# A new order for attention and a mixture of adapters, with three pairs of pieces stored as one

## The chip, the core and the metric

The kernel runs on one core of one Trainium2 chip. The metric is the device time of one execution in microseconds; the median of four executions before the change is 254.44 us (254.34 to 254.68). A second number is the span of a profiled execution, from the first to the last instruction.

A core has five instruction streams. PE (TensorE) multiplies matrices, DVE (VectorE) and ACT (ScalarE) work on tiles and copy results out of PSUM, POOL (GpSimd) here issues the loads, and SP (SyncE) issues the stores. The 16 DMA engines of the core move the data; loads and stores have a queue each and share these engines.

## The reference, cut to what matters

Four batches of 6400 rows and 256 columns. Attention is taken across the columns: the Gram matrix of k and q over all 6400 rows of a batch, divided by the norms of the columns, goes through a softmax and gives a 256x256 matrix `a`; each row of v is multiplied by it. The result goes through eight small adapters of rank 16, of which each row takes its best two.

```python
qn = q / (np.linalg.norm(q, axis=1, keepdims=True) + 1e-06)
kn = k / (np.linalg.norm(k, axis=1, keepdims=True) + 1e-06)
s = kn.transpose(0, 2, 1) @ qn / tau
a = np.exp(s - s.max(-1, keepdims=True))
a /= a.sum(-1, keepdims=True) + 1e-09
x = (v @ a).reshape(B * S, D)
...
logits = x @ w_gate
topk = np.argpartition(-logits, K, axis=1)[:, :K]      # K = 2
w = softmax of the two logits
x + sum over the two of w * ((x @ A[e]) @ B[e])
```

## The kernel before

**Tiles.** A batch's 6400 rows lie as 128 partitions times 50 rows ("columns" of 256 numbers, 1 KB in DRAM, 512 bytes in SBUF since the loads convert to bf16). q and k are loaded in three parts of 17, 17 and 16 columns (`QK`), the first part of batch 0 with four columns ahead on other queues, and some parts in two transfers (`PARTS`). v is loaded in five pieces of 10 columns. There are six buffers for parts of q and k, three for pieces of v, four for transposed v (`vT`), and seven for results (`y`), each of one piece (`STORE`).

**Stages of a batch.** For each of the 50 columns, PE adds k's column times q's column to the Gram matrix in PSUM (L593). The squared norms come in one of two ways, by groups of columns: with PE as two more matmuls of 128 columns (L597 for k, L602 for q), or, for the groups listed in `OFF`, with ACT squaring (L615), DVE adding (L621, L627, L630) and a small matmul at the end (L636). A chain of short steps follows: diagonals (L663), an inverse square root (L677 to L693), scaling (L705, L710), exp (L715), sum and transposes (L722 to L735), the product of `a` with the gate and adapter weights (L742 to L757), and `a` itself (L763).

**Pieces.** Each piece of v is transposed by PE (L788) and copied to `vT`. Gate logits and the adapters' first products come in one of two ways: merged, in one run of 136-column matmuls (L812) that is copied out to `zl` before the gate can be worked out, for the pieces in `MERGED`; or apart, with 8-column matmuls for the logits first (L826) and 128-column matmuls for the products later (L879). DVE finds the two best in eight short steps (L845 to L868, one of ACT among them), multiplies (L890), PE transposes again (L902), and the output of two columns at a time is four matmuls of vT with `a` (L915) and two of the adapters' second weights (L920). ACT or DVE copies it to `y` (L769, L771). A store moves a piece of `y` to DRAM (L928); the last two pieces go out in three stores each (`FINE`).

**What sets the order.** Nothing is scheduled on the chip. `make_plan` writes down every step with an engine, or a choice of two, its cost in microseconds, its dependences, a rank, and the buffers that it takes and gives back. `Plan.run` plays them through: at each moment each engine takes the step of the lowest rank that is ready, loads go out in the order of `WORDS` as soon as their buffer is free, and two DMA queues share the bandwidth. The order in which it started the steps is the order in which the program is recorded, engine by engine. So every constant of that play (`LAT`, `ISSUE`, the costs in `make_plan`, `Clock` for PE's clock) can move any instruction. `warm` steps are matmuls of zeros (L777) that it puts in where PE has nothing to do.

**Queues.** POOL issues the loads one after another (L578): a load that waits for its buffer holds up all loads behind it. The buffer of a part of q or k is free when its Gram columns and squares are done, that of a piece of v when its last transpose is done. SP issues the stores in one order too. `HOLD` keeps some stores back until a load has landed, so that loads have the DMA to themselves: before the change by a small transfer into `scrap` that reads the loaded tile (L645), behind which the later stores stand.

The loads of the kernel before follow `WORDS` after the three parts of batch 0 ("q11" is the second part of q and k of batch 1, "v03" the fourth piece of v of batch 0):

```python
WORDS = ('q10 v00 v01 v02 q11 v03 q12 v04 v10 v11 q20 v12 v13 v14 q21 v20 v21 v22 q22 q30 '
         'q31 q32 v23 v24 v30 v31 v32 v33 v34')
```

## Time and profile before

| | |
|---|---|
| Median of four executions | 254.44 us |
| The profiled execution's own time | 254.68 us |
| Its span | 252.9 us |
| Mean granted TensorE clock | 0.975 |
| POOL's loads of v waiting for PE's transposes | 119.5 us in 12 waits |
| Instruction fetch (queue q8) | 18 packets, 0.29 MB |
| A v load of 640 KB, issue to landing, median | 18.1 us |
| A y store of 1280 KB, issue to landing, median | 16.8 us |
| First load of 512 KB (q, issued at 0.00) | 3.9 us |

How to read the profile's rows: busy time is given for each engine with its share of the span and the number of instructions. The rows of digits cut the span into 40 slices; a 9 means 90% or more. In the tables by stage the columns are the stretch, its length, the busy time of each engine with its number of instructions, the granted share of PE's clock, the mean busy share of the 16 DMA engines (packets overlap a little, so a full stage shows slightly over 1) and the bytes that they moved per time. A load counts there with the bytes that it writes to SBUF, half of what it reads. In the chain of waits a row is a start, a length and what it was. In the table of waits a row is who waited, for what, and then the sum, the number and the longest.

### The profile page before, as it was taken

The numbers are of one execution on the slowest core, as the hardware profiler recorded it, in microseconds if no ns is written. First come the engines' busy times: TensorE is split into PE (matmuls) and PEld (weight loads), VectorE is DVE, ScalarE is ACT, GpSimd is POOL, SyncE is SP. The second block draws the span as 40 slices with busy tenths as digits, with TensorE's granted clock in tenths as the row PEclk, the third lists the DMA queues.
The fourth block names the chain that finished last, engine by engine and source line by source line (L and its number), as shares of the span: only waits on it lengthen the run. The fifth ranks groups of instructions, "written<-read, shape, count | busy, mean of one in ns | idle before, by whom it ended". The sixth has DMA issues, their size and how long they took to land.

```text
span 252.9 us, 5852 instructions
## 1 busy us (share of the span) xinstructions
PE 221.4 (88%) x2357; PEld 195.1 (77%) x2357; DVE 192.8 (76%) x528; ACT 151.0 (60%) x269; POOL 27.0 (11%) x54
## 2 busy tenths in 40 slices
PE   0275997988999998989999999889999979999990
PEld 0163882776899998789899899779999768999980
DVE  0055589768988996888899898589898898888840
ACT  5454427444876665785667758362674846657670
POOL 7003010040002002000500100500000000000000
PEclk9999798699999999999999999999999999999998
DMA  8999999999999999999999999999999999999995
GB/s 252 217 217 209 212 221 214 212 219 212 218 215 217 316 284 295 264 212 222 211 213 220 216 217 213 216 210 321 312 253 353 330 330 323 339 390 426 399 405 225
DMA packets 11243, 66.70 MB, mean 264 GB/s; under 512 B 1360, under 2 KB 1744, under 8 KB 6608
## 3 DMA queue, kind: packets, MB, share of 16 engines
q0 software_dynamic: 6912, 38.80, 74.3%
q1 hardware_dynamic: 3968, 26.87, 26.1%
q10 hardware_dynamic: 336, 0.66, 0.7%
q8 instruction: 18, 0.29, 0.4%
q14 instruction: 9, 0.07, 0.1%
HBM read 78.91 MB, written 26.21 MB: 416 GB/s over the span
## 4 chain that ended last, share of the span: by engine, by line
PE 72%; DMA 12%; DVE 9%; ACT 2%; issue 2%; POOL 2%; DVEq 0%; POOLq 0%
PE Y_ps L915 17%; PE acc L593 14%; DMA qk<-in_k_dram 12%; PE Y_ps L920 8%; PE T_ps L788 7%; PE ZL_ps L812 6%; PE gzT_ps L902 5%; PE acc L597 4%; PE acc L602 3%; PE warm_ps L777 2%; PE n2p_ps L636 2%; DVE a_bf L763 2%; POOL qk L578 1%; PE Z_ps L879 1%; PE log_ps L826 1%
## 5 line engine op out<-in xcount | busy, mean ns | idle before, releaser
L593 PE MATMUL acc<-qk 128*128 128x256 bf16 x400 | 71.7, 289 | 16.3 <-DMA qk<-in_k_dram 9.1
L915 PE MATMUL Y_ps<-a_bf,vT 128*128 128x256 bf16 x400 | 60.0, 272 | 0.2 <-DVE acc_sb L710 0.2
L621 DVE TENSOR_TENSOR ssq<-ssq,sq 128x1280 f32<-128x1280 f32 (+1 forms) x27 | 43.4, 1606 | 19.6 <-ACT sq L615 19.6
L769 ACT COPY y<-Y_ps 128x512 f32<-128x512 f32 x79 | 46.1, 586 | 17.5 <-PE Y_ps L920 14.4
L593 PEld LDWEIGHTS <-qk 128*128 128x128 bf16 x400 | 35.3, 104 | 20.7 <-DMA qk<-in_k_dram 10.8
L615 ACT ACTIVATE sq<-qk 128x1280 f32<-128x1280 bf16 (+1 forms) x27 | 36.9, 1367 | 17.5 <-DVE ssq L621 16.6
L915 PEld LDWEIGHTS <-vT 128*128 128x128 bf16 x400 | 39.0, 98 | 4.7 <-issue 0.3
L920 PE MATMUL Y_ps<-ball,gzT 128*128 128x256 bf16 x200 | 38.2, 273 | 0.0
L597 PE MATMUL acc<-qk 128*128 128x128 bf16 x242 | 34.9, 226 | 0.0
L769 ACT COPY vT<-T_ps 128x512 f32<-128x512 f32 (+1 forms) x44 | 21.2, 510 | 12.8 <-PE T_ps L788 12.4
L788 PE MATMUL T_ps<-ident,v 128*128 128x128 f32 x200 | 27.5, 274 | 0.6 <-DVE waA_sb L757 0.4
L597 PEld LDWEIGHTS <-qk 128*128 128x128 bf16 x242 | 24.7, 102 | 3.9
L890 DVE TENSOR_TENSOR gz<-zl,gateg 128x256 bf16<-128x256 f32 x70 | 26.4, 445 | 0.3
L578 POOL DMA_DIRECT2D v<-in_v_dram x20 | 11.5, 575 | 132.8 <-PE T_ps L788 119.5
L602 PE MATMUL acc<-qk 128*128 128x128 bf16 x168 | 23.6, 223 | 0.0
L788 PEld LDWEIGHTS T_ps<-ident,v 128*128 128x128 f32 x200 | 22.3, 141 | 1.6 <-DVE waA_sb L757 0.6
L902 PE MATMUL gzT_ps<-ident,gz 128*128 128x128 f32 x100 | 20.9, 281 | 2.6 <-DVE gateg L868 1.4
L920 PEld LDWEIGHTS <-gzT 128*128 128x128 bf16 x200 | 19.6, 98 | 2.3
L812 PE MATMUL ZL_ps<-waA_sb,vT 128*128 128x136 bf16 x280 | 19.5, 223 | 1.7 <-DVE waA_sb L757 1.5
L812 PEld LDWEIGHTS <-vT 128*128 128x128 bf16 x280 | 17.7, 98 | 2.4 <-issue 2.1
L771 DVE COPY gzT<-gzT_ps 128x256 f32<-128x256 f32 (+1 forms) x40 | 15.0, 379 | 4.7 <-PE gzT_ps L902 3.1
L771 DVE COPY y<-Y_ps 128x512 f32<-128x512 f32 x21 | 14.5, 700 | 4.1 <-PE Y_ps L920 4.1
(80 smaller groups left out, 271.2 us busy)
## 6 DMA issues: line engine op xcount, KB each, us to landing
out_dram<-y SPq DMA_DIRECT2D x18, 1280.0 KB, 16.8
v<-in_v_dram POOLq DMA_DIRECT2D x20, 640.0 KB, 18.1
qk<-in_q_dram POOLq DMA_DIRECT2D x7, 1088.0 KB, 20.1
qk<-in_k_dram POOLq DMA_DIRECT2D x7, 1088.0 KB, 26.0
qk<-in_q_dram POOLq DMA_DIRECT2D x4, 512.0 KB, 19.4
qk<-in_k_dram POOLq DMA_DIRECT2D x4, 512.0 KB, 22.7
qk<-in_q_dram POOLq DMA_DIRECT2D x2, 1024.0 KB, 18.7
qk<-in_k_dram POOLq DMA_DIRECT2D x2, 1024.0 KB, 23.0
```

The lines of the kernel that those rows point to most:

```text
L593: nc.tensor.matmul(acc[ic][:, 0:256], kt[:, j, ic::CC], qt[:, j, :], start=c == 0, stop=False, skip_group_check=True)
L597: nc.tensor.matmul(acc[ic][:, 256:384], kt[:, j, ic::CC], kt[:, j, ic::CC], start=False, stop=False, skip_group_check=True)
L602: nc.tensor.matmul(acc[ic][:, 384:512], qt[:, j, ic * P:(ic + 1) * P], qt[:, j, ic * P:(ic + 1) * P], start=False, stop=c == NC - 1, skip_ ...
L615: nc.scalar.activation(out[:, 0:n, :], t[:, j:j + n, :], ACT.Square)
L621: nc.vector.tensor_tensor(out=t, in0=t, in1=held["sq", (w, b, g), ""][:, 0:n, :], op=OP.add)
L769: nc.scalar.copy(out, in_)
L771: nc.vector.tensor_copy(out, in_)
L788: nc.tensor.matmul(ps[:, j, :], vt[:, c + j, :].bitcast(FP32), W["ident32"], is_transpose=True, start=(j == 0), stop=(j == n - 1))
L812: nc.tensor.matmul(ps[:, j, :], vT_of(b, i, c + j)[:, :, ic], st[b]["waA"][:, ic, :], start=(j == 0 and ic == 0), stop=(j == n - 1 and ic ...
L902: nc.tensor.matmul(ps[:, j, :], pairs[:, j * P:(j + 1) * P], W["ident32"], is_transpose=True, start=(j == 0), stop=(j == n // 2 - 1))
L915: nc.tensor.matmul(ps[:, j, :], vT_of(b, i, c + j)[:, :, ic], st[b]["a"][:, ic, :], start=(j == 0 and ic == 0), stop=False, skip_group_che ...
L920: nc.tensor.matmul(ps[:, j, :], pair[:, :, j], W["B"], start=False, stop=(j == 1), skip_group_check=True)
```

## The change

The change does five things.

1. The play of the plan is another. DMA is no longer two streams that share by size: each transfer is eight rows per engine, two rings take turns row by row, a few rows are fetched ahead, and a landing takes longer the later it is. Costs of steps are other numbers, `Clock` uses other thresholds, and `HEAD`, the time at which software loads begin to move, is 5.05 instead of 2.6.
2. With it the constants of the order are others: `WORDS`, `HOLD`, `OFF` (31 entries instead of 35), `MERGED` (8 pieces instead of 14), `AHEAD`, `SQ`, `SAFE`.
3. `y` and `v` are each one tile with slots in place of a tile for each buffer, so that two neighbouring slots can be read by one store.
4. `PAIRS`: pieces 0 and 1 of batch 0, 0 and 1 of batch 1, and 2 and 3 of batch 2 lie in neighbouring slots and are stored in one transfer of 20 columns each, 20 KB per partition.
5. A held store has a dependence on the load itself (`add_manual_dep`) and the transfers into `scrap` are gone.

What is computed is the same: the same matmuls, with other pieces merged and other groups of squares on PE or on ACT and DVE. The loads keep their sizes; four columns of q and k of batch 0 go ahead as before.

```diff
-    WINDOW, FIRST, LOW, HIGH = 3.413, 0.31, 0.5, 0.8
+    WINDOW, FIRST, LOW, HIGH = 3.413, 0.31, 0.4, 0.8
...
-    SPARE = 1.0
+    SPARE = 1.5
...
-    LAT = 0.07
-    DMA_LAT = 1.8
+    TAIL = {"PE": 0.164, "DVE": 0.083, "ACT": 0.1}
+    LAT = 0.037
     ENGINES = ("PE", "DVE", "ACT", "POOL", "SP")
-    ISSUE = 0.55
-    ISSUE_LAT = 1.8
-    STORE_LAT = 1.4
+    ISSUE, ISSUE_LAT = 0.52, 1.8
+    STORE, STORE_LAT = 0.46, 0.85
     OUT = 8
+    PIPE, FETCH = 2.9, 1.005
+    ROW, SEM = (0.003, 0.012), (0.021, 0.006)
+    DMA_LAT, SPREAD, SKEW = 0.31, 0.6, 0.008
...
+        def fill():
+            nonlocal turn, ahead
+            while ahead < self.PIPE and (rings[0] or rings[1]):
+                turn = 1 - turn if rings[1 - turn] else turn
+                s = rings[turn][0]
+                if s.rows:
+                    s.rows -= 1
+                    us, last = s.size * self.FETCH + self.ROW[turn], None
+                else:
+                    rings[turn].pop(0)
+                    us, last = self.SEM[turn], s
+                pipe.append((us, last))
+                ahead += us
...
+PAIRS = {(0, 0), (1, 0), (2, 2)}
...
+def pieces(b, i):
+
+    return next((((b, j), (b, j + 1)) for j in (i - 1, i) if (b, j) in PAIRS), ((b, i),))
...
-    for kind, b, i in sorted(set(HOLD.values())):
-        part = [k for k in p.steps if k[:4] == ("load", kind, b, i)]
-        p.add(("hold", kind, b, i), {"SP": 0.3}, part[-1:], 0, size=0.01)
...
-WORDS = ('q10 v00 v01 v02 q11 v03 q12 v04 v10 v11 q20 v12 v13 v14 q21 v20 v21 v22 q22 q30 '
-         'q31 q32 v23 v24 v30 v31 v32 v33 v34')
-HEAD = 2.6
-LOAD = 0.304
+WORDS = ('v00 q10 v01 q11 v02 q12 v03 q20 q21 v04 v10 v11 q22 v12 v13 q30 v14 q31 v20 v21 v22 q32 v23 v24 v30 '
+         'v31 v32 v33 v34')
+HEAD = 5.05
+COL = 1.024 * 1.17647 / 32
 WARM = 150
-AHEAD = 2.7
+AHEAD = 3.4
...
+HOLD = {(0, 0): ('k', 3, 0), (0, 1): ('v', 0, 4), (0, 2): ('v', 3, 3), (0, 3): ('v', 3, 4), (1, 0): ('v', 2,
+        3), (1, 1): ('k', 1, 1), (1, 2): ('v', 2, 4), (1, 3): ('v', 3, 2), (1, 4): ('k', 3, 1), (2, 4):
+        ('v', 3, 3), (3, 2): ('v', 2, 3), (3, 3): ('v', 0, 1), (3, 4): ('k', 2, 1)}
...
+MERGED = {(0, 1), (0, 4), (1, 1), (1, 3), (1, 4), (2, 1), (2, 3), (2, 4)}
...
+    Y = sbuf.tile([P, STORE["y"] * PC, C], FP32, name="y")
+    VS = sbuf.tile([P, STORE["v"] * PC, C], BF16, name="v")
...
     def do_store(s, b, i, c, n):
         lo = i * PC + c
-        nc.sync.dma_start(out_v[b, :, lo:lo + n, :], held["y", (b, i), ""][:, c:c + n, :])
+        at_y = at["y", (b, i)] * PC + c
+        p = 0
+        for rows in SHARES if (b, i) in SPLIT else (P,):
+            r = nc.sync.dma_start(out_v[b, p:p + rows, lo:lo + n, :], Y[p:p + rows, at_y:at_y + n, :])
+            if (b, i) in HOLD and not p:
+                tc.add_manual_dep(r.ins, loaded[held_by(plan, b, i)],
+                                  mybir.DependencyInfo(mybir.DependencyClass.Sync, mybir.DependencyReason.DATA),
+                                  reason="held")
+            p += rows
```

In the program that this makes, SP's stores come in this order (batch.piece; in brackets the load whose landing a store is held for): 0.4; the pair 0.0 and 0.1 [k of q30]; 1.4 [k of q31]; 2.0; the pair 1.0 and 1.1 [v23]; 1.2 [v24]; 2.1; the pair 2.2 and 2.3; 1.3 [v32]; 0.2 [v33]; 2.4 [v33]; 0.3 [v34]; 3.0; 3.1; 3.2; and 3.3 and 3.4 in three stores each. Before it was 0.2; 0.1 [k of q12]; 0.3; 0.0 and 1.0 [k of q31]; then 2.0, 0.4, 1.1, 1.2, 1.3, 1.4 and 2.1 [k of q31 or q32]; 2.2 to 3.2 one by one; and 3.3 and 3.4 in three each. PE has 2357 matmuls before and 2506 after, of them 39 and 12 on zeros; the last eight pieces' outputs stand behind the last Gram matmul before, and the last seven after. DVE has 48 instructions fewer, ACT 22 more.

## The prediction

> **What bounds the kernel now.** I read the page first, then the busy time by stages, the chain of waits and the waits of the loads' queue.
>
> ```profile
> span 252.9 us, 5852 instructions
> ...
> PE 221.4 (88%) x2357; PEld 195.1 (77%) x2357; DVE 192.8 (76%) x528; ACT 151.0 (60%) x269; POOL 27.0 (11%) x54
> ...
> DMA  8999999999999999999999999999999999999995
> ...
> q0 software_dynamic: 6912, 38.80, 74.3%
> q1 hardware_dynamic: 3968, 26.87, 26.1%
> ...
> HBM read 78.91 MB, written 26.21 MB: 416 GB/s over the span
> ```
>
> The row DMA is full in every slice but the first and the last, and the two queues add up to 100.4% of 16 engines' span. No instruction engine comes near that. Loads read 78.9 MB and stores write 26.2 MB whatever the order, so a new order can win only idle DMA time, or lose more of it. The chain of waits gives PE 72%: PE works nearly all the time too, but not on the tightest resource. Where is the DMA idle? By stages:
>
> ```profile
> core 0: us, PE busy (x) PEld busy (x) DVE busy (x) ACT busy (x) POOL busy (x), PEclk, DMA share, GB/s
> ...
> 10.00:80.00 70.00, 59.22 (x543) 47.73 (x544) 50.29 (x113) 40.79 (x57) 8.46 (x15) 0.93 1.04 215
> 80.00:105.00 25.00, 24.15 (x273) 21.92 (x271) 21.33 (x65) 14.65 (x28) 2.94 (x6) 1.00 1.03 292
> ...
> 225.00:235.00 10.00, 10.00 (x130) 9.51 (x128) 9.10 (x29) 6.82 (x17) 0.00 (x0) 1.00 1.02 427
> 235.00:240.00 5.00, 5.00 (x58) 4.60 (x55) 4.36 (x15) 3.28 (x8) 0.00 (x0) 1.00 0.92 384
> ...
> 245.00:250.00 5.00, 1.55 (x15) 1.14 (x12) 0.00 (x0) 1.96 (x4) 0.00 (x0) 1.00 0.97 385
> 250.00:253.00 3.00, 0.00 (x0) 0.00 (x0) 0.00 (x0) 0.00 (x0) 0.00 (x0) 0.57 0.11 44
> ```
>
> GB/s counts the SBUF side: 215 for loads alone (430 read from HBM), 427 for stores alone. Only 235:240 (0.92), and the run-out after 245, fall short. A piece of v (0.655 MB in SBUF) thus costs 0.655/215 = 3.05 us of all engines, a 17-column part of q or k 5.18, a 16-column part 4.88, a 10-column store 1.311/427 = 3.07.
>
> **The change part by part.** Order of instructions by engine in the two programs, priced by rows of this trace:
>
> PE. Pitches from the chain of waits:
>
> ```profile
> 218.80 1.18 PE ZL_ps L812 x20
> ...
> 226.01 1.12 PE Z_ps L879 x20
> 227.13 0.48 PE log_ps L826 x20
> ...
> 245.89 0.44 PE Y_ps L915 x4
> 246.59 0.58 ACT y L769
> ```
>
> Six more pieces take gate logits and Z apart instead of merged: 6 x (0.48 + 1.12 - 1.18) = +2.5 us. OFF has 31 entries instead of 35: 56 more 128-column matmuls, at 0.06 each (two L597 rows start 0.12 us before the next line's): +3.4. So +5.9 us of needed work; 27 fewer warm-up matmuls of 0.22 (-5.9) only filled idle time. Two Y rows start 0.655 us apart. With such pitches the needed work is 199.4 us before and 205.1 after.
>
> DVE. Rows by shape: additions of squares -6 x 1.754 + 2 x 1.487 = -7.5; evictions of merged results -8 x 0.434 - 7 x 0.580 = -7.5; gzT handed to ACT -15 x 0.420 - 7 x 0.285 = -8.3; y handed to ACT -7 x 0.700 = -4.9; vT -1.6: about -30 of 192.8. ACT takes up those and gives squares back (-6.8): +3. Neither bounds the whole; both can delay PE locally.
>
> Last stretch of PE. Behind the last Gram matmul stand 47.1 us of PE work before (its Gram matmuls ended at 194.9, its last y eviction began at 246.59: 4.6 us of stalls) and 43.1 after, since eight pieces' Y stood behind it and now seven do.
>
> Pairs. Three transfers fewer of unchanged bytes. Cost of a row: median packets of 10 KB took 398 ns and of 2 KB 84, so the part that does not scale is 84 - 398/5 = 4 ns; 3 x 8 rows per engine give 0.1 us. Bounds 0 (bytes alone) and -0.3 (three times as much a row); I take -0.1.
> [...]
> A store row twice as long also holds loads up. In 80:105, with loads l and stores s, l + s = 292 and 2l + s = about 425: l = 133, s = 159, a ratio of 1.2, like row sizes 10.2 KB to 8.7 KB. With 20.5 KB rows the ratio would be 2.35: l = 98, s = 230. A pair of 2.62 MB takes 11.4 us, in which loads fall 35 x 11.4 = 0.40 MB or 1.9 us behind and regain it. It costs time only if PE waits for just that load; 0 to 1.9, I take 0.
> [...]
>
> SP. Three scrap transfers go (three issues of 0.5 us), and a held store waits for its load's semaphore itself. What queues behind it are only later stores; DVE or ACT wait for them where a y slot is still full. Holds now reach further: pieces 2 and 3 of batch 0 go out after the last two loads have landed, so after the loads a larger store backlog covers the last stretch of PE. That fills the dip in 235:240: (427 - 384) x 5 / 427 = -0.5 us (0 to -0.5). The run-out: 385 x 5 + 44 x 3 = 2.06 MB is 4.8 us at 427, and took from 245 to about 251.9: 2.1 us lost. With 4 us less PE work behind the last Gram I take back a third: -0.6 (0 to -1.3).
>
> POOL. v waits dominate its queue, 119.5 us in all:
>
> ```profile
> POOL v L578 <- PE T_ps L788: 119.5, 12, 27.1
> ...
> 78.70 0.53 POOL L578 DMA_DIRECT2D v<-in_v_dram  x1 [17.72 <-PE T_ps L788]
> ```
>
> They cost nothing while something moves. At 78.70 there was cover: SP's first stores were issued at 78.83. After the change the order is v00 q10 k10 v01 q11 k11 v02 q12 k12 v03 q20 k20, then q21. From the landing of batch 0's last load (35.2 in the chain) those make 4 x 3.05 + 6 x 5.18 + 2 x 4.88 = 53.0: the queue is empty at about 88, for the engines that are ahead a microsecond sooner. q21 takes the slot of q01's successor and must wait for batch 1's Gram columns 17 to 33; every store before is held or not computed, so nothing would cover. PE: the first gate logits began at 57.25; I take 56, since one addition of 1.75 no longer stands before rsqrt. From there to that Gram column PE has 25.4 us of matmuls (28 Gram columns 10.0, 11 Y steps 7.2, the rest 8.2): 81.4, and with stalls of 12%, as between 57.25 and 108.39 before (45.0 us of work in 51.1), 84.5. Issue to first data: 512 KB landed 3.9 us after the first issue, 1.2 of it moving, so 2.7: 87.2. Against 87 to 88 that is a gap of 0 to 0.3; if PE runs at half clock for one more stretch, 3. I take +0.2, bounds 0 to 3. It is the tightest place.
>
> Code. 298 more PE matrix and weight instructions at 18 fetches of 16 KB so far: about one fetch, +0.05 us; on one engine, near the end, up to 0.9.
>
> Sum: -0.5 - 0.6 - 0.1 + 0.2 + 0.05 = -0.95. The profiled execution took 254.68 (span 252.9 and 1.8 around it), 0.24 over the median of 254.44; so 253.73 for its like and **253.5** as a median. The forecast's own range is 253.0 to 253.9.
>
> **The rivals.**
> Loads run dry (slower): the place above. If batch 1's Gram column 33 ends after 84.8 (87.5 - 2.7), each microsecond is lost to the DMA and never regained. 3.3 us more stalls give a gap of 3 in place of 0.2: 253.5 + 2.8 = 256.3. For it: 10:80 has PE at 59 of 70 us with the clock granted at 0.93, and there are fewer warm-ups; against it: 30 us less on DVE. It decides from a gap of 1.2 us, where the gain is gone.
> PE becomes the bound (slower): piece 4 of batch 0 lands at 88 + 10.4 + 3.05 = 101.5, 136.8 us of PE work stand from its transposes on. Before, 129.9 took 108.39 to 246.59, 6.4% stalls. With 3% PE ends at 242.4, with 6% at 246.5 as now, with 7% at 247.9; the 5.3 us from the last y eviction to the last store's end follow as before, so 7% is 1.3 later: 255.7. It decides from 6%. For it: +5.9 us of work; against it: less DVE, and PE has Gram columns between dependent steps.
> DMA as full as before, nothing won: the dip closes but the run-out is the same and q21 costs 0.4: 254.4. For it: the row DMA.
> Larger gain: the store backlog lasts through PE's end, run-out at its bound of -1.3, pairs -0.3: 252.6.
>
> **How the numbers follow.** Forecast 0.43, larger gain 0.10, nothing 0.13, loads dry 0.20, PE bound 0.14. Faster by over 0.2% (0.5 us, about what a measurement of this kernel tells from no change): 0.53; within: 0.13; slower: 0.34. The range from 252.6 to 256.5 (the loads' rival and a little more) leaves about 2 in 10 outside, mostly longer droughts.
>
> **What would show it.** DMA share without a dip from 80 to 95 and from 235 to 245; the last y eviction at 247 or sooner; a GB/s of 400 or more from 245 until the last store; DVE near 163, PE needed work up and its warm-ups 12; the pairs' rows at the same GB/s as single ones. An issue of q21 after 85, or any slice of the row DMA under 9 between the second and the last but one, would make the prediction wrong.

## The result, and the profile after

The changed kernel takes 255.21 us in the median of 39 executions (254.26 to 256.87), the kernel before 254.55 in 60 (254.11 to 255.74) on the same chips. The ratio is 1.0026, with a 95% interval of 1.0017 to 1.0034: slower by a quarter of a per cent, where the forecast was 253.5, faster. The time lies in the range 252.6 to 256.5; the direction is wrong. The best executions of the two kernels are alike (254.26 and 254.11); the changed one has a tail: 10 of 39 executions lie over 255.5, of the kernel before 1 of 60. Executions over 1.5% above the fastest of their kernel are not counted here or below, which concerns two of the eight of run e4.

The profiled execution took 256.22 us, one of that tail. Its page:

```profile
span 254.4 us, 6064 instructions
...
PE 225.4 (89%) x2506; PEld 202.2 (79%) x2506; DVE 161.8 (64%) x480; ACT 152.4 (60%) x291; POOL 26.2 (10%) x54
...
PEclk9959799599999999999999999999999769999997
DMA  8999999999999999999999999999999999999996
GB/s 250 211 219 209 214 218 216 217 213 214 219 213 218 218 215 209 218 219 208 272 263 216 322 315 212 211 251 279 214 350 380 354 256 182 399 418 422 424 391 241
...
q1 hardware_dynamic: 3440, 26.87, 25.6%
...
q8 instruction: 20, 0.33, 0.5%
```

DVE has lost 31 us of work, and the row DMA is still full of nines. The row GB/s tells more: 256 and 182 in the slices of about 203 to 216 us, where loads and stores are mixed, and PEclk has a 7 and a 6 in the slices from 197 to 210. The busy time by stages (columns: stretch, length, busy time of each engine, granted clock, DMA share, GB/s):

```profile
200.00:205.00 5.00, 4.44 (x27) 4.31 (x28) 3.90 (x21) 3.64 (x8) 0.53 (x1) 0.56 1.04 381
205.00:210.00 5.00, 5.00 (x39) 4.73 (x37) 3.18 (x13) 3.60 (x10) 0.53 (x1) 0.75 0.95 216
210.00:215.00 5.00, 4.21 (x66) 3.81 (x65) 5.00 (x16) 3.92 (x10) 0.53 (x1) 1.00 1.04 195
...
235.00:240.00 5.00, 5.00 (x57) 4.50 (x56) 2.38 (x8) 3.51 (x7) 0.00 (x0) 1.00 1.01 428
```

The dip of 235:240 is closed (428 in place of 384 GB/s), as forecast. But with a load's byte counted twice, since it is read as fp32 and lands as bf16, the packets of 205 to 220 move 360, 383 and 364 GB/s in place of about 425: some 2 us of DMA time lost. The DMA share hardly shows it (0.95 to 1.04). Why no more was in the queue is in the table of waits (who waited for what: sum, number, longest), in the order of time and in the chain of waits:

```profile
DVE y L812 <- DMA out_dram<-y: 6.3, 2, 4.4
...
ACT y L810 <- DMA out_dram<-y: 2.1, 1, 2.1
```

```profile
191.23 1.29 DVE L812 COPY y<-Y_ps 128x512 f32<-128x512 f32 x2 [4.35 <-DMA out_dram<-y]
...
199.93 1.07 ACT L810 COPY y<-Y_ps 128x512 f32<-128x512 f32 x2 [2.12 <-DMA out_dram<-y]
...
200.00 1.29 DVE L812 COPY y<-Y_ps 128x512 f32<-128x512 f32 x2 [1.95 <-DMA out_dram<-y]
...
200.56 0.96 PE L685 MATMUL n2p_ps<-ones,ssqq 128*128 128x1 f32 x4 [1.61 <-ACT y L810]
```

```profile
183.02 16.88 DMA out_dram<-y
...
199.93 0.59 ACT y L810
...
200.56 0.96 PE n2p_ps L685 x4
```

No y eviction waits for a store in the kernel before. Here the pair of pieces 1.0 and 1.1, issued at 183.02 once its load (v23) has landed, takes until 199.62 (its last packet; its semaphore comes at 199.90), and piece 2.2 is to be evicted into its slots. Both evicting engines stand still until then, PE's banks stay full, and batch 3's norm of q gets no bank: PE stops at 198.95, right behind the last Gram, until 200.56, and goes on at half clock. (The longer wait of 4.35 us at 191.23 is in every split kernel too, and PE does not stop there: it is busy for 4.99 of the 5 us from 190 to 195.) So piece 2.3, and with it the pair 2.2 and 2.3, is late: SP issues this pair at 213.68, while the store ahead of it (2.1) had landed at 207.7. From 207.7 until then only loads move, and v33 and v34 too are issued late, as they wait for PE's transposes.

### The profile page after: what moved, and what is told of

Same layout as the page of the kernel before. It is cut to its first block, busy times and chain, and to the rows that moved or that the text cites. A ratio compares the mean times of both kernels' runs of the same rounds, so it can differ in the third digit from the quotient of the medians.

```text
span 254.4 us, 6064 instructions
## 1 busy us (share of the span) xinstructions
PE 225.4 (89%) x2506; PEld 202.2 (79%) x2506; DVE 161.8 (64%) x480; ACT 152.4 (60%) x291; POOL 26.2 (10%) x54
## 4 chain that ended last, share of the span: by engine, by line
DMA 40%; PE 39%; DVE 11%; ACT 4%; issue 2%; POOL 2%; ACTq 0%; POOLq 0%
DMA qk<-in_q_dram 19%; PE Y_ps L955 8%; DMA v<-in_v_dram 8%; DMA out_dram<-y 7%; DMA qk<-in_k_dram 7%; PE T_ps L828 6%; PE acc L642 5%; PE Y_ps L960 4%; PE Z_ps L919 4%; PE gzT_ps L942 3%; PE ZL_ps L852 2%; DVE ssq L670 2%; PE acc L646 2%; PE log_ps L866 2%; PE acc L651 2%
## 5 line engine op out<-in xcount | busy, mean ns | idle before, releaser
L642 PE MATMUL acc<-qk 128*128 128x256 bf16 x400 | 76.9, 286 | 13.7 <-DMA qk<-in_k_dram 6.4
L670 DVE TENSOR_TENSOR ssq<-ssq,sq 128x1280 f32<-128x1280 f32 (+1 forms) x23 | 35.8, 1556 | 29.8 <-ACT sq L664 29.5
L642 PEld LDWEIGHTS <-qk 128*128 128x128 bf16 x400 | 36.9, 103 | 17.3 <-DMA qk<-in_k_dram 7.5
L955 PEld LDWEIGHTS <-vT 128*128 128x128 bf16 x400 | 37.8, 98 | 3.9
L664 ACT ACTIVATE sq<-qk 128x1280 f32<-128x1280 bf16 (+1 forms) x23 | 30.5, 1325 | 16.0 <-DVE ssq L670 8.6
L646 PE MATMUL acc<-qk 128*128 128x128 bf16 x240 | 35.4, 231 | 0.0
L651 PE MATMUL acc<-qk 128*128 128x128 bf16 x226 | 32.9, 229 | 0.0
L646 PEld LDWEIGHTS <-qk 128*128 128x128 bf16 x240 | 25.1, 105 | 4.5 <-issue 0.2
L664 ACT ACTIVATE ssq<-qk 128x1536 f32<-128x1536 bf16 (+1 forms) x8 | 11.5, 1435 | 23.8 <-DMA qk<-in_q_dram 15.3
L930 DVE TENSOR_TENSOR gz<-Z_ps,gateg 128x256 bf16<-128x256 f32 x60 | 22.0, 439 | 2.4 <-PE Z_ps L919 2.1
L651 PEld LDWEIGHTS <-qk 128*128 128x128 bf16 x226 | 20.0, 103 | 0.6
L810 ACT COPY gzT<-gzT_ps 128x256 f32<-128x256 f32 (+1 forms) x42 | 13.3, 337 | 11.0 <-PE gzT_ps L942 10.6
L919 PE MATMUL Z_ps<-waA_sb,vT 128*128 128x128 bf16 x240 | 17.6, 219 | 0.0
```

The source lines that it names most:

```text
L642: nc.tensor.matmul(acc[ic][:, 0:256], kt[:, j, ic::CC], qt[:, j, :], start=c == 0, stop=False, skip_group_check=True)
L646: nc.tensor.matmul(acc[ic][:, 256:384], kt[:, j, ic::CC], kt[:, j, ic::CC], start=False, stop=False, skip_group_check=True)
L651: nc.tensor.matmul(acc[ic][:, 384:512], qt[:, j, ic * P:(ic + 1) * P], qt[:, j, ic * P:(ic + 1) * P], start=False, stop=c == NC - 1, skip_ ...
L664: nc.scalar.activation(out[:, 0:n, :], t[:, j:j + n, :], ACT.Square)
L670: nc.vector.tensor_tensor(out=t, in0=t, in1=held["sq", (w, b, g), ""][:, 0:n, :], op=OP.add)
L810: nc.scalar.copy(out, in_)
```

## The experiments

All are copies of the changed kernel in which the plan's order is kept and only what is named is edited, so that nothing else moves. "Mean over before" is the mean of the executions less that of the kernel before, measured beside them on the same chip, with 1.96 standard errors.

| run | edit | median, us | mean over before | over 255.5 |
|---|---|---|---|---|
| first runs | changed kernel | 255.21 | 0.65 +- 0.22 | 10 of 39 |
| e6, e10, e16 | the same again | 254.66, 255.19, 255.31 | 0.55, 0.53, 0.71 | 9 of 36 |
| e1 | third pair split | 254.93 | 0.24 +- 0.27 | 1 of 12 |
| e2, e11 | second pair split | 254.57, 254.87 | 0.07, 0.35 | 3 of 24 |
| e12 | second and third split | 254.83 | 0.39 +- 0.27 | 1 of 11 |
| e3, e13 | all pairs split | 254.70, 254.82 | 0.12, 0.34 | 1 of 24 |
| e14 | all split, 6.0 us less PE | 254.67 | 0.30 +- 0.37 | 1 of 12 |
| e15 | all split, 6.3 us more PE | 254.64 | 0.12 +- 0.18 | 0 of 11 |
| e4 | store 0.2 early | 257.38 | 2.35 +- 1.28 | 4 of 6 |
| e5 | PE's stall filled | 254.82 | 0.51 +- 0.35 | 3 of 12 |
| e7 | second pair without hold | 254.79 | 0.56 +- 0.40 | 3 of 12 |
| e8 | 3.2 us less PE | 255.06 | 0.75 +- 0.54 | 3 of 12 |
| e9 | kernel before again | 254.35 | -0.12 +- 0.16 | 0 of 11 |
| e17 | all split, last semaphore | 254.76 | 0.11 +- 0.23 | 0 of 11 |
| e18 | pairs kept, last semaphore | 254.63 | 0.08 +- 0.31 | 1 of 12 |

### Is it the pairs' transfers? (e1 to e4)

The split stores the named pair as two transfers, in the pair's place on SP:

```diff
     for s in steps:
-        do[s.key[0]](s, *s.key[1:])
+        if s.key[0] == "store" and s.key[1:3] in SPLIT_PAIRS:
+            b, i = s.key[1:3]
+            do_store(s, b, i, 0, PC)
+            do_store(s, b, i, PC, PC)
+        else:
+            do[s.key[0]](s, *s.key[1:])
```

with `{(2, 2)}` in e1, `{(1, 0)}` in e2 and all three in e3; e4 emits the store of 0.2 ahead of the pair 2.2 and 2.3, without its hold.

> Edit: of the changed kernel, only the third pair (pieces 2.2 and 2.3) is stored as two transfers of 10 columns in the pair's place; every other instruction and its order stay. In the changed kernel SP's next store behind 2.1 (landed about 207.7 us) is this pair, and it issues only at 213.68 because it waits for the last eviction of 2.3; that of 2.2 was done near 201. Theory A (the end is set by DMA, and the drought of about 2.0 us at 205 to 220 is the loss): the first half issues near 202, no window from 205 to 220 stays under about 400 GB/s equivalent, and the time falls by 1 to 2 us, to 253.3 to 254.2. Theory B (PE's chain of batch 3 sets the end: the stall at 198 to 201 and the clock after it): the drought closes as in A, but the last y eviction stays within 0.4 us of 249.1 and the time within 0.4 us of the changed kernel's. Theory C (PE's added work, +5.7 us of matmuls, sets the end whatever the stores do): the same time, as in B; e2 and e3 part B from C.

> Edit: only the second pair (pieces 1.0 and 1.1, slots 5 and 6) is stored as two transfers of 10 columns, both held as before. In the changed kernel this pair is issued at 183.02 and lands at 199.62, and the evictions of piece 2.2 into slot 5 wait for that (ACT 2.12, DVE 1.95 us), with batch 3's norms behind them. Theory B (that wait starts PE's stall and the cold clock of 200 to 210): the first half lands near 195, the two waits go or fall under 0.5 us, the granted clock in 200:210 is over 0.85, batch 3's logits come 1.5 to 3 us earlier than 214.4 and the time falls by 0.8 to 2.5 us. Theory A: the wait goes, but the drought of the pair 2.2 and 2.3 moves with it, and the time falls by under 0.8. Theory C (PE's work): the waits go, PE waits elsewhere instead, and the time stays within 0.4 us. A fourth, D (a bundle at the row level: two 10-column stores take more packets than one of 20): the time rises, by under 0.2.

> Edit: all three pairs are stored as two transfers of 10 columns each, in the pair's place; the order, the slots and the holds of the changed kernel stay. It undoes the pairs as transfers and leaves the new order. If the pairs' transfers are what costs (A and B together), the time is under the kernel before's, 252.5 to 254.2. If the new order with its added PE work costs (C), it is within 0.4 us of the changed kernel's 255.2. If pairs help by fewer packets (what they were worth in the prediction: 0.1 us for three), it is 0.1 us above the changed kernel's, which these rounds can hardly show.

> Edit: the store of piece 0.2 (its data lie ready in slot 2 since batch 0; the changed kernel holds it until load v33 has landed and issues it at 214.68) is issued without its hold ahead of the third pair on SP, so near 194 behind 2.1. All three pairs stay. It fills the gap in the stores, 207.7 to 216, with 1.28 MB and changes nothing in PE's, DVE's or ACT's waits. Theory A (DMA drought): the windows of 205 to 215 rise by 100 GB/s or more and the time falls by 1 to 2 us. Theory B and C (PE's chain, or PE's work): the time stays within 0.3 us, or rises by up to 0.5 because v31 and v32 share the rows with this store and land later.

In e2 the first half lands at 194.70. The wait of piece 2.2 is gone from the order of time, and in the busy time by stages PE works through 195:205 at full clock:

```profile
197.91 1.08 ACT L810 COPY y<-Y_ps 128x512 f32<-128x512 f32 x2
...
198.14 1.28 DVE L812 COPY y<-Y_ps 128x512 f32<-128x512 f32 x2
```

```profile
195.00:200.00 5.00, 5.00 (x54) 4.74 (x52) 4.56 (x20) 2.63 (x6) 0.00 (x0) 1.00 1.04 317
200.00:205.00 5.00, 5.00 (x52) 4.38 (x51) 4.59 (x25) 4.48 (x12) 1.06 (x2) 1.00 1.03 389
```

In e1 the stall stays, as its table of waits shows, but the first half of the pair goes out at 201.9 and its busy time by stages has 328 GB/s in 205:210; up to 220 no DMA time is lost (0.04 us by the sum used below), though a dip is back in 235:240 (374 GB/s):

```profile
DVE y L812 <- DMA out_dram<-y: 6.5, 2, 4.5
...
ACT y L810 <- DMA out_dram<-y: 2.1, 1, 2.1
```

```profile
205.00:210.00 5.00, 5.00 (x48) 4.52 (x47) 5.00 (x19) 4.31 (x12) 0.84 (x2) 1.00 1.03 328
```

e2's ratio is 1.0000 (0.9987 to 1.0013), e3's 1.0004 (0.9993 to 1.0014), e1's 1.0011 (0.9997 to 1.0024). Either end of the chain, the wait at its start or the gap in the stores at its end, can be taken away, but no split kernel reaches the 253 us that theories A and B had allowed: their last packets (251.26 to 251.35) are near the kernel before's (251.86, and 251.52 in e9).

e4 is a clear miss for theory A. It fills the gap (328 GB/s in 205:210) and makes the time longer: the ratio to the kernel before is 1.0092 (1.0051 to 1.0133). Its busy time by stages follows below. The 1.31 MB take DMA time from the loads: v33 lands at 221.6 and v34 at 229.3 (after: 214.7 and 219.6), PE waits for their pieces, and the store is missing from the backlog at the end (0.74 of DMA's time in 240:245):

```profile
205.00:210.00 5.00, 5.00 (x50) 4.51 (x48) 5.00 (x19) 4.32 (x11) 0.75 (x2) 1.00 1.03 328
...
220.00:225.00 5.00, 3.31 (x28) 3.28 (x29) 0.99 (x3) 1.45 (x3) 0.00 (x0) 0.77 0.98 341
...
240.00:245.00 5.00, 5.00 (x62) 4.70 (x60) 2.19 (x6) 3.52 (x7) 0.00 (x0) 1.00 0.74 298
```

This hold of the changed kernel earns its place: in e4 the fuller DMA (328 GB/s in place of 216 in 205:210) was worth nothing, since it moved what nobody waited for.

### Stall, clock, hold or PE's work? (e5 to e8)

e5 puts 14 matmuls of zeros into unread columns of the bank of k's norm, ahead of q's; e7 skips the hold of (1, 0); e8 skips k's norm matmuls for `5 <= c < 12`, so that its output lacks that part of the norm; e6 has no edit.

> Edit: the changed kernel with 14 more matmuls of zeros (128x256, about 0.11 us each, 1.5 us in all) on PE, between batch 3's last Gram chunk and the norm of q that waits for a bank (198.7 to 200.56 in the profile of the changed kernel, after which the clock is granted at 0.56 and 0.75 for 10 us). They write columns nobody reads. The pairs, the slots and all waits stay. Theory B1 (the loss is the clock that follows the stall): the windows 200:205 and 205:210 have a clock of 0.95 or more in the profile and the median falls by 0.3 to 0.8 us, to 254.4 to 254.9, with the executions over 255.5 gone. Theory B2 (the stall itself, 2 us on batch 3's chain, is the loss, and the clock is by the way): the median stays within 0.2 us of the changed kernel's. Theory C (PE's work sets the end): it rises by 0.5 us or more, as this adds 1.5.

> The changed kernel once more, unedited, beside the others on one chip, for the spread of its time and a second profile. Its 39 runs so far lie between 254.26 and 256.87 and those of the kernel before between 254.11 and 255.74. If the clock after the stall makes that spread (B1), a profile of an execution under 255 shows the same waits for the pair's store near 198 to 200 but a clock of 1.0 at 200:210, and one over 255.5 a clock under 0.8 there. If the stores' drought makes it (A), the two differ in the GB/s of 205:215 at the same clock.

> Edit: only the hold of the second pair (pieces 1.0 and 1.1, until load v23 has landed) is taken away; it stays one transfer of 20 columns in its place on SP. It then issues right behind store 2.0, near 181.6 in place of 183.02. Theory B (the wait of piece 2.2 for this transfer): the store ahead of it still lands near 191, and the pair's bytes run behind it, so slots 5 and 6 come free 0 to 1.4 us earlier than 199.6; the stall shrinks by at most that and the median falls by 0 to 0.4 us. If the hold is the main cost and not the transfer's length, the median falls by all of the 0.6 to 0.8 us that the kernel with the pair split has gained. Theory C: no change.

> Edit: the changed kernel leaves out the matmuls of k's norms for chunks 5 to 11 of each batch: 56 matmuls of 128x128, at a pitch of 0.113 us 6.3 us of PE's work, about what the change added (5.7). That part of the norm is missing from the output. Stores, pairs, slots and order stay. Theory C (the added work on PE sets the end): the median falls by 0.6 us or more, under 254.6. Theory B (the wait for the pair's store): the last Gram comes earlier but the evictions of piece 2.2 still wait until 199.6, the stall on PE gets longer by what the Gram is earlier, and the median stays within 0.3 us of the changed kernel's in the same call.

e6 was the telling one. Its profile is of an execution of 254.47 us of the same program, with the same waits (DVE 5.7, ACT 1.4 us) and a stop of PE in the same place, though a shorter one (0.87 us against 1.61), and in its busy time by stages the clock stays up:

```profile
200.00:205.00 5.00, 4.93 (x49) 4.43 (x50) 4.72 (x27) 4.99 (x14) 1.05 (x2) 1.00 1.02 383
205.00:210.00 5.00, 5.00 (x54) 4.62 (x53) 5.00 (x17) 4.25 (x10) 0.53 (x1) 1.00 1.06 249
210.00:215.00 5.00, 4.21 (x70) 3.91 (x68) 4.72 (x22) 3.59 (x13) 0.00 (x0) 1.00 1.08 271
```

The pair 2.2 and 2.3 is issued at 210.2, a microsecond after 2.1 has landed, and no DMA time is lost. All eight profiles of kernels with the pairs kept and the plan's SP order fall into two groups. "Lost" is, from 70 to 220 us, 150 less the bytes moved (loads twice) over 425 GB/s:

| run | time | PE waits for q's norm bank | PE busy in the clock window | clock in 200:205 | pair 2.2 issued | lost | last packet |
|---|---|---|---|---|---|---|---|
| after | 256.22 | 1.61 | 0.53 | 0.56 | 213.7 | 1.88 | 253.02 |
| e16 | 256.19 | 2.01 | 0.41 | 0.67 | 212.3 | 1.25 | 252.33 |
| e7 | 255.73 | 2.00 | 0.53 | 0.79 | 212.5 | 1.28 | 252.53 |
| e10 | 255.40 | 1.89 | 0.45 | 0.66 | 212.7 | 1.45 | 252.07 |
| e8 | 254.96 | 1.81 | 0.65 | 1.00 | 210.8 | 0.25 | 251.75 |
| e18 | 254.84 | 1.47 | 0.63 | 1.00 | 210.5 | -0.02 | 251.11 |
| e5 | 254.78 | filled | 0.99 | 1.00 | 210.7 | 0.22 | 251.48 |
| e6 | 254.47 | 0.87 | 0.74 | 1.00 | 210.2 | -0.08 | 251.06 |

Where the clock goes down behind the stall, the pair is issued at 212.3 to 213.7 in place of 210.2 to 210.8, and what the DMA loses shows nearly in full in the last packet. The length of the stall alone does not tell the groups apart: 1.61 us was followed by half the clock in the first profile, 1.81 us by the full clock in e8. The traces show what goes with it. In each of them the granted clock changes only at times that are whole multiples of 3.413 us apart, and these windows lie at another place of the program from one execution to the next (one ends at 200.65 in the first profile, one at 199.49 in e8). The fourth column is PE's busy share of the window that holds most of the stall. In the four profiles where one window holds all or most of the stall and is busy for 0.41 to 0.53, the next was granted half the clock; in e8 the stall of 198.88 to 200.69 is divided by a window's end at 199.49, and neither window is busy for less than 0.65. In these eight profiles the clock thus goes with both, how long PE stands and where the windows happen to fall; what sets it was not shown, and elsewhere the share does not go with it, as the last section tells. Over 76 executions of the unedited kernel the time goes with the mean granted clock (correlation -0.52; -0.96 within e6, -0.13 within e10), over the 59 of e2, e3, e11, e12 and e13 it does not (-0.05).

That the clock alone is the cost was not shown, though: in e5 the zeros keep PE busy (1.69 us of them in the trace) and the clock at 1.00 in its profile, and yet 3 of 12 executions lie over 255.5 and the mean has not moved. What those three lost was not profiled; B1 stays open as the whole story. e7 gives nothing (200.1 in place of 199.6 for the pair's last packet, though it is issued 1.3 us earlier): the transfer's length and place are at fault, not the hold. In e8 PE's work was 3.2 us less, not the 6.3 of its expectation, since 0.113 us holds two such matmuls; the median stayed, which speaks for B.

### The same on one chip, and PE's work (e9 to e16)

> The kernel before once more, unedited, for a second profile and the spread of its own time beside the others on one chip: a ratio to itself of 1.000 within 0.001, no execution over 255.8. The prediction took the dip of 235:240 (384 GB/s in the first profile) for a loss of 0.5 us of every execution. If that is so, this profile shows 375 to 395 GB/s there again; if it belongs to one execution, over 410 and a last packet near 251.3 in place of 251.86.

> The changed kernel once more, unedited, beside the kernel with the second pair split on one chip. Theory B: a median of 254.6 to 255.2, a mean 0.4 to 0.7 us over the kernel before's, and at least 2 of 12 executions over 255.5, with a lower clock than the others'. Theory C and the theory that no part of the change costs anything on this chip: the spread is that of the kernel before.

> The second pair (1.0 and 1.1) split once more, on the same chip as the changed kernel itself. Theory B (that pair's 16.6 us from issue to landing holds slots 5 and 6 and with them batch 3's chain): a median within 0.2 us of the kernel before's, at most 1 of 12 executions over 255.5, and a mean 0.3 to 0.6 us under the changed kernel's in this call. If the first result was the chip's and not the edit's, the two have the same mean within 0.2 us.

> The second and the third pair are split, the first stays. Theory B: as with the second alone, within 0.2 us of the kernel before's. Theory A on top of it (the third pair's wait for piece 2.3 leaves the stores empty-handed for a moment even without the stall): 0.1 to 0.3 us better than the second alone, which would put it at or under the kernel before's median. If neither kernel can get under the bytes (105.1 MB at the 424 GB/s of the full windows are 248 us behind the first load), all of these end at 251.0 to 251.4 at best.

Here theory B was only half right. e11 has 1.0017 (1.0006 to 1.0028) and e12 1.0019 (1.0007 to 1.0031), with no stall and no drought in their profiles; e10 has 1.0019 (1.0004 to 1.0034), and its two executions over 255.5 had clocks no lower than the others' (0.959). Between e10 and e11 the means differ by 0.19 +- 0.39, where 0.3 to 0.6 was expected. Together, the unedited kernel's 75 timed executions lie 0.63 +- 0.17 over the kernel before and the 59 with the second pair split 0.25 +- 0.12: the split is worth 0.38 +- 0.21, and 0.25 remain. Not all of the 0.38 is the wait for the pair, as the last of these sections shows. e9 shows 402 GB/s in 235:240, so the dip is smaller there than in the first profile (384); by the bytes moved (loads twice) since 70 us the kernel before is behind by 0.76 and 0.64 at 240, so most of the loss is in both profiles.

> All three pairs split once more, beside the unsplit kernel and beside less and more PE work on one chip. If the transfers of 20 columns cost about half of the loss (so the means so far: 0.24 us over the kernel before with the second pair split, 0.57 without), its mean is 0.1 to 0.4 us over the kernel before's and 0.2 to 0.5 under the unsplit one's. If the pairs cost nothing, it has the unsplit one's mean within 0.1 us.

> All three pairs split, and k's norms left out for chunks 1 to 11 and 34 to 36 of every batch: 112 matmuls of 128x128; two of them take 0.113 us in the timeline, so 6.3 us of PE's work (the earlier run e8 left out 56, thus 3.2 us and not the 6.3 that its expectation named). That part of the norm is missing from the output. Theory C (the added work on PE is the rest of the loss): the mean falls to the kernel before's, within 0.1 us, or under it. Theory D (the rest belongs to the transfers' order and the lag of one DMA engine): the same mean as e13 within 0.15 us.

> All three pairs split, and 4 more matmuls of zeros (128 columns each) for chunks 5 to 11 of every batch: 112 matmuls at 0.0565 us, 6.3 us more for PE, some 1.6 us per batch. Theory C: as 5.7 us of added work would have cost 0.25 us or more, another 6.3 cost at least 0.3 us more than e13, and over 1 us if PE has no room left in batch 3. Theory D: PE waits for loads in the Gram of each batch and takes the work there; the same mean as e13 within 0.15 us.

> The changed kernel, unedited, beside these three. A mean 0.4 to 0.7 us over the kernel before's, with at least 1 of 12 executions over 255.5; if its profile has a clock under 0.9 in 200:210, it also has under 200 GB/s in 210:215 and a last packet after 252; if its clock there is 1.0, a last packet before 251.8.

e14 skips k's norms also for `1 <= c < 5` and `34 <= c < 37`, which its output lacks (106 matmuls less by its page and 6.0 us, not the 112 and 6.3 of its expectation, as batch 3's last three are on ACT and DVE already); e15 adds four matmuls of zeros per chunk to the accumulators. The page has PE's busy time at 217.7 us in e14, and in e15 at

```profile
PE 227.3 (90%) x2618; PEld 205.2 (81%) x2618; DVE 161.7 (64%) x480; ACT 152.3 (60%) x291; POOL 26.2 (10%) x54
```

Neither differs from e13 in time (1.0010, 1.0004 and 1.0008, all within 0.9994 to 1.0026). Theory C falls: 6.3 us more on a PE that is busy for 88% of the span cost nothing that can be measured (the means of e15 and e13 differ by -0.21 +- 0.28). e16 repeats the unedited kernel's loss: 1.0028 (1.0010 to 1.0045), 5 of 12 over 255.5, last packet 252.33, as expected of a profile with a low clock. Its stages:

```profile
200.00:205.00 5.00, 4.14 (x31) 4.02 (x32) 4.30 (x22) 4.02 (x9) 0.53 (x1) 0.67 1.04 383
205.00:210.00 5.00, 5.00 (x49) 4.67 (x48) 4.10 (x17) 4.44 (x13) 0.62 (x2) 0.99 0.98 220
210.00:215.00 5.00, 4.21 (x76) 3.82 (x74) 4.96 (x16) 3.48 (x11) 0.44 (x1) 1.00 1.03 190
```

### What was left: SP's closing waits (e17, e18), and time outside the span

From the last store's packet to the end of the span the kernel before takes 1.04 and 1.05 us (first profile and e9), the changed one 1.42 to 1.55, the split ones 1.24 to 1.41. At the end SP waits for nine pairs of semaphores in a fixed order, 0.06 us each. These are the starts of SP's records, in us:

```
before  last packet 251.86 | ... 248.47 249.10 250.32 251.56 252.19  drain 252.25
after   last packet 253.02 | 250.13 252.73 253.36 253.43 253.49 253.55 253.61 253.67 253.73  drain 253.79
e18     last packet 251.11 | ... 247.74 248.36 249.60 250.83 251.46  drain 251.52
```

In the traces of both kernels the transfers on SP take the semaphores in turn. In the kernel before the last store happens to have the one that SP waits for last, and the other eight waits are over by then. The changed kernel makes six transfers fewer there (three pairs, three scrap transfers), so its last store has the third, and six waits come behind it. The table of SP's own waits shows it too, with five closing waits that a store still ends in the kernel before, then two in the changed one:

```profile
SPq L982 <- DMA out_dram<-y: 4.2, 5, 1.2
```

```profile
SPq L1030 <- DMA out_dram<-y: 3.1, 2, 2.5
```

e17 and e18 add tiny transfers at the start so that the last store is the ninth again:

```diff
+        if s.key[:3] == ("store", 0, 4):
+            for n in range(6):
+                nc.sync.dma_start(scrap[:, 2 * n + 2:2 * n + 4], W["ident"][0:1, 2 * n:2 * n + 2])
```

(3 in e17, with all pairs split.)

> All three pairs split, and 3 transfers of 4 bytes on SP at the start, so that the last store has the semaphore that SP waits for last (27 transfers on SP from there on, as many as the kernel before makes). Theory E (the closing waits are the rest of the loss): from the last packet to the end of the span 1.0 to 1.1 us in place of 1.24, and a mean 0.15 to 0.25 us under the split kernel's 0.23 over the kernel before, so -0.05 to 0.1 us against the kernel before. Without E: the same 0.2 to 0.3 us over it.

> The changed kernel with its pairs, and 6 transfers of 4 bytes on SP at the start, so that the last store has the semaphore that SP waits for last. The stall of piece 2.2 and the clock stay as they were. Theory E: from the last packet to the end of the span 1.0 to 1.1 us in place of 1.42, the fastest execution at or under 254.0 (unedited: 254.26), and the mean 0.2 to 0.35 us over the kernel before's (unedited: 0.63), with executions over 255.3 still there from the stall. Without E: a mean of 0.5 us or more over it.

Both take 1.06 us from the last packet to the end. In e18 the five are back:

```profile
SPq L1039 <- DMA out_dram<-y: 4.1, 5, 1.2
```

e18's ratio is 1.0000 (0.9988 to 1.0013), its fastest executions, 253.97 and 254.00, lie under every one of the unedited kernel's, and five of 12 lie over 254.8: the stall is still there (1.47 us in its profile), though two of the five are long only by time outside the span, as told below. e17 has 1.0005 (0.9996 to 1.0014). Theory E is confirmed for the piece it names; the means (0.08 +- 0.31 and 0.11 +- 0.23) can't tell whether anything is left. Nor do they tell the pairs apart from the split ones: with the closing waits alike, e18 and e17 differ by -0.03 +- 0.37. No version is faster than the kernel before by what can be measured.

One more part of the loss is neither stall nor closing wait. An execution's time is its span and something outside it. In all 159 executions of the kernel before that were measured beside e1 to e18 this is 1.73 to 1.86 us, 1.79 in the mean; in the 76 of the changed kernel the mean is 1.97, with 24 over 2.0 and a highest of 2.89. Five of the twenty profiles (e4, e6, e16, e17, e18) have an instruction fetch of 16 KB (queue q8) that starts 1.0 to 1.8 us behind the end of the span; the others have none there. In e4, e6, e16 and e18 the time outside is 1.88, 1.97, 2.44 and 2.66 us, each time 0.24 us less than from the span's end to the end of this fetch; in e17, where the fetch ends sooner, it is 1.78 as in the profiles without one. The program before is fetched in 18 such pieces, the changed one in 20, and in e8, e14 and e15, which have 56 and 106 matmuls less and 112 more, all 35 executions stay within 1.74 to 1.84. So the late fetch fits to 0.01 us; no edit was made for it alone. With it go e18's 254.84 and e16's 256.19 in the table above, which are longer than their last packets suggest, and five of the 20 executions of the changed kernel over 255.5 would lie under it with 1.79 us outside.

The mean loss of the changed kernel can so be split: 0.18 +- 0.06 us are outside the span, and the closing waits of its four profiles are on average 0.41 us longer than before. That is nearly all of the 0.63. In the kernels with the second pair split the same parts are 0.08 and 0.27 of 0.25. Without both, the span is 0.04 us longer than before with the pairs and 0.10 shorter with the second pair split; these 0.14 +- 0.19 us are what is left in the mean for the wait for the pair.

## Why the prediction was wrong

- **The step that failed** is the one on SP: "What queues behind it are only later stores; DVE or ACT wait for them where a y slot is still full", priced at nothing, and with it the pairs' "0 to 1.9, I take 0". The price was looked for at the loads; it was at the slots. A pair of 2.62 MB frees its two slots only when all of it has landed, here 16.6 us after its issue, and is issued only when both pieces are done. The slot's next users stood in ACT's and DVE's order ahead of batch 3's norms, so PE stopped for 0.9 to 2.0 us, and where the clock went down behind it the DMA lost 1.2 to 1.9 us. In the mean over executions this is the smaller part: splitting the pairs gained 0.38 +- 0.21 us, of which 0.14 +- 0.19 remain when closing waits and the time outside the span are taken out.
- **A term that was missing in the same step**, and the largest in the mean: the transfers that go were counted as three issues of 0.5 us won. That their number sets which semaphore the last store has was not considered: 0.37 to 0.50 us in each of the changed kernel's four profiles (1.42 to 1.55 against 1.04 and 1.05), and e18, which sets only this right, has a ratio of 1.0000.
- **Code, +0.05, "on one engine, near the end, up to 0.9"**: two fetches more, not one, and one of them near or behind the end. The bound was the right place to look: the time outside the span grew by 0.18 us in the mean and by 1.1 in one execution.
- **The dip, -0.5**: right in size. At 240 us the kernel before is 0.64 to 0.76 behind the full rate, e6 0.02, the profiles with the second pair split (e2, e3, e11, e12, e13) 0.04 to 0.37.
- **The run-out, -0.6**: mis-sized by all of it. From 240 on, 3.90 MB are left in e6, 9.18 us at 425 GB/s; it takes 11.06, a loss of 1.9. The same sum gives 2.0 and 1.7 for the kernel before in its two profiles and 1.7 to 2.7 for those five split ones. Nothing was won there.
- **q21, +0.2**: it was issued at 81.30, not 84.5, and the slices from 76 to 95 stay at 215 to 218 GB/s. That rival (0.20) falls, and with it "the tightest place". Neither of the two signs that were to show the prediction wrong came: a late q21, or a slice of the row DMA under 9. The busy share stayed at 0.95 to 1.04 while 2 us were lost.
- **PE as the bound** (0.14): falls with e14 and e15. The +5.9 us were there and hidden. Behind the last Gram PE stood still or ran at half clock for 7.0 us in the profile after (198.95 to 249.09, less 43.1 of work), against 4.6 before, and the last y eviction was over at 249.7, but for another reason than the added work.
- **"27 fewer warm-up matmuls ... only filled idle time"**: not settled. No stall of the kernel before was followed by a clock under 1.00 in 185 to 245 in its two profiles; e5's zeros did not bring the mean back.
- **DVE near 163**: 161.8. **Pairs -0.1**: too small for any of these runs to show in the time; in the profile after, the median row of 20 KB takes 761 ns on its engine and two of 10 KB 770.

In a good execution (e6) the last packet comes 0.5 to 0.8 us earlier than before and the closing waits take 0.4 back, which leaves little that can be measured; in a bad one the drought of 1.2 to 1.9 us, the late fetch, or both come on top. That the best executions of both kernels are alike is a balance of these, not a sign that nothing changed.

## What to carry to other kernels

Before stores are joined, ask who gets their buffers next: the transfer's time from issue to landing (16.6 us for the second pair here) is the time that all of its slots are shut, and its issue waits for the last of its pieces (the third pair's until 213.68 us). Where DMA is full for nearly the whole span, as here (38 of 40 slices at 90% or more), an order can win little and lose more; look for the stall that lets a queue run empty once, and judge a change by the spread of its times, not by one profile. Take the time outside the span apart from the span: a tail need not come from the schedule. And look at the last microsecond: the order in which the closing waits are made was worth 0.4 us here, almost half of what the whole new order was to win.

## What the runs showed of the hardware

- In all 20 traces the granted clock changes only at times that are whole multiples of 3.413 us apart. The stop of PE behind batch 3's last Gram was followed by half the clock for one or two such windows in four profiles (6.8 us in the first, 3.4 us in e7, e10 and e16; stops of 1.6 to 2.0 us, PE busy for 0.41 to 0.53 of the window) and by 1.00 in four (e1, e6, e8 and e18: 0.9 to 1.8 us, 0.63 to 0.74), in the same stretch of the same order. It was not so everywhere: split kernels kept 1.00 behind windows near 215 us that were busy for 0.44 to 0.54 (e12, e14, e13, e1, e3), for which no reason was found.
- The 16 DMA engines don't finish a load together in these traces: the first load's completion marks lie 0.4 to 1.3 us apart (0.94 in the profile after), and by the ninth load 1.2 to 2.4 (1.33), and it stays at 1.2 or more until the last four loads. In e11 (255.31 us) it was 2.36, in e2, the same program, 1.50 (254.47): from the fifth load to the 28th (120 us) each landed 0.7 to 0.9 us later, and the last packet came 0.82 later, with no drought in either; that the one brings the other was not tested. The kernel before has it too (0.71 us at the first load, 1.80 at the ninth).
- A closing wait on SP whose semaphore was already there took 0.06 us (six of them from 253.43 to 253.79 in the profile after).
- In four profiled executions (e4, e6, e16 and e18) an instruction fetch of 16 KB ran behind the last instruction, and the time outside the span was 1.88 to 2.66 us, up to 0.9 over the usual 1.78, each time 0.24 us less than from the span's end to the fetch's end.
